# The eight constants of the 32nd-key pick move from the value products' PSUM bank to the score tile, and the pick moves one place forward

## The chip, the cores and the metric

The kernel runs on one core of one Trainium2 chip. Its engines are TensorE (PE in the profile; its weight loads are listed as PEld), VectorE (DVE), ScalarE (ACT), GpSimd (POOL) and SyncE (SP, which issues most DMAs). Each takes its own instructions in the order in which they were written and waits on semaphores for the others. The metric is the device time of one execution in microseconds (us), as the median over runs.

## The reference

Attention over 8 batches and 8 heads of 576 tokens with 64 dimensions, in which each query keeps its 32 best keys, and behind it a layer of 8 experts over the 4608 tokens:

```python
scores = scale * np.matmul(q, k.transpose(0, 1, 3, 2))
kth = np.partition(scores, -top_k, axis=-1)[..., -top_k:-top_k + 1]   # top_k = 32
scores = np.where(scores >= kth, scores, -1000000000.0)
attn = softmax(scores); attn_out = np.matmul(attn, v)
# then, for each token x: expert = argmax of cosine logits, gate = its softmax weight
out[mask] = gate_w[mask, None] * (np.maximum(x[mask] @ w1[e], 0.0) @ w2[e])
```

## The kernel before

The attention works in 32 units (a unit is one head of a pair of batches) of 9 tiles of 128 queries, 288 tiles in all, each against 576 keys. A loop (line 1026) writes out one iteration i for each tile, and every engine's order is that in which the loop writes. One tile passes through the engines over several iterations:

- `nat(i + 2)` (line 737): PE multiplies queries and keys of tile i+2 into the score tile `sc`, two PSUM banks of which columns 0 to 287 are written. There is one such tile. Right behind it `evac(i + 2)` (line 741) has ACT copy it to SBUF as `xs`.
- `groups(i)` and `chain(i - 1)` (lines 746, 754): DVE takes the eight largest of each of 8 groups of 72 scores (8 MAX8, line 750), and from these 64 the best 24 (lines 763 to 769, the last result is `z`).
- `sign1(i - 2)` (line 772): ACT compares all scores with the 24th value of the groups and counts, in `c1`, how many lie above it. `below(i - 2)` (line 779): POOL multiplies scores and signs into `y2`, where the values still to be searched are the largest.
- `select(i - 3)` (line 784), the pick: DVE takes the next eight from `y2` (line 789), and line 790 picks the one of them that is the 32nd key. To that end it compares `c1` with eight constants, `winp`, and adds up the products into `tall`.
- `sign2(i - 4)` (line 803): ACT compares the scores with the picked value; `offset(i - 5)` (line 813): DVE makes the mask `r` of it.
- `chunk` (line 823): for the unit before, PE computes the transposed scores of 128 keys in `pt` and adds the masks; ACT takes the exponential into `w` (line 859). `av` (line 862): PE multiplies one or two such `w` with the values, adding up in `po`, a PSUM bank of its own, in 6 of 9 iterations. `norm` (line 881): twice in 9 iterations ACT copies `po` to SBUF as `ob` (line 891).

Within iteration i ACT's order is: squares for the expert layer where there are any, `sign1`, `norm`'s copy, a copy of an expert block where there is one, `sign2`, `evac`, exponential. PE's is: `nat`, `chunk`, a small product for the expert logits in some, `av`, pieces of early expert blocks. DVE's is `offset`, then `groups` and `chain` taken in turn, the pick's two instructions set among them by the number `SEL`, as lines 1099 to 1107 say. A planner (SLOT and ROOM, lines 999 to 1013) hands PE, ACT and POOL additional pieces where it reckons them free; from about 390 us on it gives PE early expert blocks.

The eight constants are a DVE copy (line 612) from SBUF. Before, they lie in columns 400 to 407 of `po`, whose columns 0 to 364 hold the value products. The framework that sets the semaphores orders all accesses of a PSUM tile by different engines, of whatever columns, and reads among them.

After the last tile (at about 915 us) the experts' layer runs, 400 us of which the change touches no line.

Of the kernel before, what the change touches and what calls it, by code (L numbers as in the profile page):

```python
# [50 lines left out]
def attn_moe_kernel(ctx: ExitStack, tc: tile.TileContext, qk, vb, vt, emb, tau, w1, w2, out):  # L51
# [537 lines left out]
    with ExitStack() as sx:  # L589
# [14 lines left out]
        sc = ps_s.tile([P, 2, 512], F32, name="sc", tag="sc")  # L604
        po = ps_s.tile([P, 512], F32, name="po", tag="po")
# [2 lines left out]
                             start=(n == 0), stop=(n == WU - 1))  # L608
        pov = po[:, 0:5 * VW].rearrange("p (t e) -> p t e", t=5)

        winp = po[:, 400:408]
        nc.vector.tensor_copy(winp, win)

        NV = 2
# [382 lines left out]
            return out_  # L997

        SLOT = 2950
        SEL = 6  # L1000
        NOSC = (2, 3)
        SQN = 1
        SQX, SCX = 600, 0
# [22 lines left out]
        while i < ntile + 12 or sideq or later or bankq or early or squares or wq or mo["seg"] \  # L1026
# [73 lines left out]
            for n in range(8):  # L1100
                mix += ga[n:n + 1]
                mix += gb[n:n + 1]
                if n == SEL:
                    mix += gc[:1]
                if n == SEL + 1:
                    mix += gc[1:]
# [436 lines left out]
    with tc.If(fv > 0):  # L1543
        with ExitStack() as sx:
# [3 lines left out]
            with tc.For_i(0, NU, 1) as u:  # L1548
# [22 lines left out]
                for ti in range(9):  # L1571
                    sc = ps_1.tile([P, 2, 512], F32, name=f"gsc{ti}", tag="pt")
# [31 lines left out]
                    po = ps_1.tile([P, D], F32, name=f"gpo{ti}", tag="pa", bufs=1)  # L1604
# [86 lines left out]
```

## Time and profile before

| | us |
|---|---|
| median of 3 runs | 1333.33 (1330.56 to 1333.66) |
| profiled execution, device time | 1337.93 |
| its span, first to last instruction | 1336.1 |
| PE busy | 1266.3 (95%) |
| DVE busy | 1058.5 (79%) |
| ACT busy | 969.6 (73%) |
| POOL busy | 834.3 (62%) |

The shares are means over two different parts. Until about 915 us attention runs and DVE is busy nearly all the time; behind it DVE is mostly idle and PE carries the experts. A busy PE is a modelled figure, since matmuls overlap. The mean granted clock of TensorE was 0.982 of full speed.

### The profile page before, as it was taken

The numbers are of one execution on the slowest core, as the hardware profiler recorded it, in microseconds if no ns is written. First come the engines' busy times: TensorE is split into PE (matmuls) and PEld (weight loads), VectorE is DVE, ScalarE is ACT, GpSimd is POOL, SyncE is SP. The second block draws the span as 40 slices with busy tenths as digits, with TensorE's granted clock in tenths as the row PEclk, the third lists the DMA queues.
The fourth block names the chain that finished last, engine by engine and source line by source line (L and its number), as shares of the span: only waits on it lengthen the run. The fifth ranks groups of instructions, "written<-read, shape, count | busy, mean of one in ns | idle before, by whom it ended". The sixth has DMA issues, their size and how long they took to land. (4 is left out here: it accounts for less than half of the span.)

```text
span 1336.1 us, 40772 instructions
## 1 busy us (share of the span) xinstructions
PE 1266.3 (95%) x14044; PEld 1113.5 (83%) x14044; DVE 1058.5 (79%) x5829; ACT 969.6 (73%) x1890; POOL 834.3 (62%) x1343
## 2 busy tenths in 40 slices
PE   6999999999889999999999999998998999999997
PEld 4888888888788898988888898887797888888896
DVE  8999999999899999999999999998524234444240
ACT  5999999999889999988899998886414234433231
POOL 5678777889977778888878889955422211123011
PEclk7999999999999999999999999999998999999999
DMA  6477455564444665656666645624363344453211
GB/s 183 127 209 209 113 129 129 139 206 111 105 118 128 174 201 167 177 160 166 165 178 197 197 129 150 174 74 162 90 208 122 123 136 144 162 175 138 79 47 36
DMA packets 137107, 195.01 MB, mean 146 GB/s; under 512 B 63143, under 2 KB 63143, under 8 KB 136754
## 3 DMA queue, kind: packets, MB, share of 16 engines
q1 hardware_dynamic: 128562, 168.97, 44.7%
q0 software_dynamic: 8192, 22.07, 5.0%
q8 instruction: 132, 2.16, 0.7%
q14 instruction: 221, 1.81, 0.4%
HBM read 115.29 MB, written 20.87 MB: 102 GB/s over the span
## 5 line engine op out<-in xcount | busy, mean ns | idle before, releaser
L750 DVE MAX8 ca<-xs 128x8 f32<-128x72 f32 x2304 | 482.4, 220 | 1.4 <-ACT xs L743 1.2
L781 POOL TENSOR_TENSOR y<-xs,s 128x576 f32<-128x576 f32 x288 | 370.3, 1287 | 116.2 <-ACT s L775 55.0
L188 PE MATMUL sc<-st 128*128 128x288 f32 x1280 | 262.3, 332 | 32.0 <-ACT xs L743 28.4
L873 PE MATMUL po<-v,w 128*64 128x73 f32 (+1 forms) x5760 | 253.2, 231 | 4.5 <-DVE jk L790 1.8
L188 PEld LDWEIGHTS sc<-st 128*128 128x128 f32 x1280 | 186.3, 192 | 71.9 <-ACT xs L743 38.2
L873 PEld LDWEIGHTS po<-v,w 128*64 128x64 f32 (+1 forms) x5760 | 220.2, 136 | 25.3 <-ACT ob L891 2.8
L775 ACT ACTIVATE s<-xs,z 128x576 bf16<-128x576 f32 x288 | 224.3, 779 | 16.0 <-DVE z L769 9.2
L858 PE MATMUL pt<-st 128*128 128x288 f32 (+1 forms) x1280 | 224.3, 297 | 0.0
L789 DVE MAX8 z<-y 128x8 f32<-128x576 f32 x288 | 213.9, 743 | 0.3 <-POOL y L781 0.3
L810 ACT ACTIVATE s<-xs,tall 128x576 bf16<-128x576 f32 x236 | 183.4, 777 | 31.6 <-DVE jk L790 26.7
L859 ACT ACTIVATE w<-pt 128x576 f32<-128x576 f32 x288 | 189.4, 658 | 20.0 <-PE pt L858 17.0
L858 PEld LDWEIGHTS pt<-st 128*128 128x128 f32 (+1 forms) x1280 | 183.8, 184 | 1.1 <-ACT s L810 0.2
L743 ACT COPY xs<-sc 128x576 f32<-128x576 f32 x288 | 180.6, 627 | 4.6 <-PE sc L188 4.2
L858 PE MATMUL pt<-negi,r 128*128 128x128 bf16 (+4 forms) x1275 | 133.9, 209 | 5.2 <-DVE r L817 4.9
L413 POOL DMA_INDIRECT out_dram<-ys_w,wi x20 | 21.4, 1068 | 170.3 <-ACT ys_w L1262 62.0
L664 POOL TENSOR_TENSOR lo<-lo,hi 128x202 fp32r<-128x202 f32 x186 | 115.4, 621 | 15.5
L858 PEld LDWEIGHTS <-r 128*128 128x128 bf16 (+1 forms) x1920 | 103.6, 99 | 23.6 <-DVE r L817 6.6
L817 DVE TENSOR_SCALAR r<-s,top 128x576 bf16<-128x576 bf16 x236 | 119.9, 508 | 0.4 <-ACT s L810 0.4
L1243 PE MATMUL ph_w<-xTh,w 128*128 128x448 f32 (+3 forms) x384 | 99.0, 340 | 7.0 <-issue 7.0
L1258 PE MATMUL py_w<-w,hh 128*128 128x512 f32 x320 | 100.1, 394 | 0.8 <-ACT ys L1262 0.8
L1247 DVE SCALAR_TENSOR_TENSOR hl<-ph_w,hh 128x448 fp32r<-128x448 f32 (+3 forms) x48 | 25.9, 540 | 67.1 <-ACT hh L1246 66.8
L1243 PEld LDWEIGHTS ph_w<-xTh,w 128*128 128x128 f32 x384 | 70.6, 196 | 10.0 <-issue 8.2
(282 smaller groups left out, 2436.9 us busy)
## 6 DMA issues: line engine op xcount, KB each, us to landing
r<-in_w SPq DMA_DIRECT2D x128, 256.0 KB
fr<-in_w SPq DMA_DIRECT2D x28, 1024.0 KB
lo<-in_qk SPq DMA_DIRECT2D x62, 304.0 KB
st<-hi SPq DMA_DIRECT2D x124, 152.0 KB
st<-lo SPq DMA_DIRECT2D x124, 152.0 KB
v<-in_v SPq DMA_DIRECT2D x32, 288.0 KB
vt<-in_vt SPq DMA_DIRECT2D x32, 288.0 KB
st<-hi SPq DMA_DIRECT2D x62, 136.0 KB
```

The costliest lines, as they stand in the source:

```text
L188: nc.tensor.matmul(sc[:, hf, :SH], qs[:, cols(b)], kk[:, b * S + hf * SH:b * S + (hf + 1) * SH], start=(n == 0), stop=(n == len(terms) - 1))
L743: nc.scalar.copy(xs.rearrange("p (a b) -> p a b", a=2), sc[:, :, :SH])
L750: return [lambda gi=gi: nc.vector.max(out=ca[:, 8 * gi:8 * gi + 8], in_=xs[:, gi * GW:(gi + 1) * GW]) for gi in range(G)]
L775: nc.scalar.activation(s1, xss[i], AF.Sign, bias=zs[i][:, 15:16], scale=-SUCC, accum_out=c1)
L781: nc.gpsimd.tensor_tensor(y2, xss[i], s1s.pop(i), ALU.mult)
L789: lambda: nc.vector.max(out=z[:, 16:24], in_=y2),
L810: nc.scalar.activation(s2s[i], xss.pop(i).rearrange("p (a b) -> p a b", a=3), AF.Sign, bias=tall[:, i:i + 1], scale=-1.0)
L817: nc.vector.tensor_scalar(r, s2s.pop(i), BIG, tops[i // 9][:, i % 9, 0:1], op0=ALU.mult, op1=ALU.max)
L858: nc.tensor.matmul(o_, l_, r_, start=start, stop=stop)
L859: nc.scalar.activation(w.rearrange("p (a b) -> p a b", a=2), ps[:, :, :SH], AF.Exp, scale=0.125)
L873: nc.tensor.matmul(o, w[:, q:q + 64], vc, start=start and n < 2, stop=stop and n in (8, 7 - b))
L1243: nc.tensor.matmul(ph, w[:, c, f * P:(f + 1) * P], x[:, c, 0:n], start=(k == 0), stop=(k == len(terms) - 1))
```

## The change

The constants are copied into columns 400 to 407 of the second bank of the score tile `sc` (row length 512, of which the scores use 288), and line 790 reads them there. `SEL` falls from 6 to 5, so that both instructions of the pick stand one MAX8 earlier among DVE's. The whole diff:

```diff
@@ -608,7 +608,7 @@
         pov = po[:, 0:5 * VW].rearrange("p (t e) -> p t e", t=5)
 
-        winp = po[:, 400:408]
+        winp = sc[:, 1, 400:408]
         nc.vector.tensor_copy(winp, win)
@@ -997,7 +997,7 @@
         SLOT = 2950
-        SEL = 6
+        SEL = 5
         NOSC = (2, 3)
```

The order of DVE's instructions around the pick of tile 141 before (names end in the tile's number; `ca144` is the eight largest of the groups of tile 144, `z141` and `y2_141` belong to the pick, `r140` is a mask):

```order
L769 MAX z143_10206<-cb143_10205 128x8 [waits DVE_49]
L750 MAX ca144_10204<-xs144_10098 128x8 x2
L789 MAX z141_10081<-y2_141_10184 128x8 [waits Pool_49]
L750 MAX ca144_10204<-xs144_10098 128x8
L790 SCALAR_TENSOR_TENSOR jk141_10207,tall_167<-po_169,c1_141_10143,z141_10081 128x8 [waits DVE_49,PE_49]
L817 TENSOR_SCALAR r140_10275<-s2_140_10213,top15_9673 128x576 [waits Activation_49]
L750 MAX ca145_10270<-xs145_10151 128x8
```

The same place of DVE in the changed kernel:

```order
L769 MAX z143_10206<-cb143_10205 128x8 [waits DVE_49]
L750 MAX ca144_10204<-xs144_10098 128x8
L789 MAX z141_10081<-y2_141_10184 128x8 [waits Pool_49]
L750 MAX ca144_10204<-xs144_10098 128x8
L790 SCALAR_TENSOR_TENSOR jk141_10207,tall_167<-sc_168,c1_141_10143,z141_10081 128x8 [waits DVE_49,Activation_49]
L750 MAX ca144_10204<-xs144_10098 128x8
L817 TENSOR_SCALAR r140_10275<-s2_140_10213,top15_9673 128x576
```

One MAX8 has gone from ahead of the pick to behind it. The pick no longer waits for PE (the value products) but for ACT, and so late an instruction of ACT, the copy of the score tile in the same iteration, that the mask behind it needs no wait for ACT of its own.

PE's order where iteration 144 begins, before (`po` is written by the value products, `sc` by the scores, `pt15_0_0` by the transposed scores of unit 15):

```order
L873 MATMUL po_169<-v0_188,w14_1_1_10028 64x73 [waits DVE_49]
L873 MATMUL po_169<-v0_188,w14_1_1_10028 64x73 x8
L873 MATMUL po_169<-v0_188,w14_1_2_10100 64x73 [waits Activation_49]
L873 MATMUL po_169<-v0_188,w14_1_2_10100 64x73 x8
L188 MATMUL sc_168<-st16_9663 128x288 [waits Activation_49]
L188 MATMUL sc_168<-st16_9663 128x288 x3
L858 MATMUL pt15_0_0_10222<-st15_9051 128x288 [waits PE_49]
```

And in the changed kernel:

```order
L873 MATMUL po_169<-v0_188,w14_1_1_10028 64x73 x9
L873 MATMUL po_169<-v0_188,w14_1_2_10100 64x73 [waits Activation_49]
L873 MATMUL po_169<-v0_188,w14_1_2_10100 64x73 x8
L188 MATMUL sc_168<-st16_9663 128x288 [waits DVE_49]
L188 MATMUL sc_168<-st16_9663 128x288 x3
L858 MATMUL pt15_0_0_10222<-st15_9051 128x288 [waits PE_49]
```

No instruction moves on PE. The wait for DVE leaves the value products and stands at the scores, where it takes the place of the wait for ACT's copy of the tile before: the pick for which PE now waits is that of the iteration before, which itself waits for that copy. On ACT the order stays as well; `ob`, the copy of `po`, waits for PE instead of DVE, and `sign2` behind it takes over the wait for DVE.

## Rows read from the trace of the kernel before

**Rows 1.** Windows: length, then busy us of PE, PEld, DVE, ACT, POOL, granted clock.
```profile
100.00:420.00 320.00, 302.32 (x4579) 273.54 (x4579) 313.99 (x1973) 293.52 (x595) 267.14 (x459) 0.99 0.52 137
420.00:880.00 460.00, 454.61 (x5696) 393.78 (x5691) 456.81 (x2776) 417.94 (x824) 381.91 (x629) 1.00 0.62 171
```

**Rows 2.** Waits of DVE in 0 to 920 us: us in total, times, longest.
```profile
DVE jk L790 <- PE po L873: 4.4, 10, 1.0
...
DVE rd L897 <- POOL rd L895: 2.2, 1, 2.2
DVE jk L790 <- PE sc L188: 1.4, 3, 0.6
```

**Rows 3.** Waits of the whole span that the change touches on PE and ACT.
```profile
PEld sc L188 <- ACT xs L743: 38.2, 48, 2.3
...
ACT s L810 <- DVE jk L790: 26.7, 87, 1.1
...
ACT ob L891 <- DVE jk L790: 12.6, 34, 0.6
```

**Rows 4.** Timeline, five iterations of the scores' weight loads: start, us, instruction.
```profile
704.05 0.56 PEld L188 LDWEIGHTS sc<-st 128*128 128x128 f32 x4
707.01 0.56 PEld L188 LDWEIGHTS sc<-st 128*128 128x128 f32 x4
710.40 0.56 PEld L188 LDWEIGHTS sc<-st 128*128 128x128 f32 x4
713.61 0.56 PEld L188 LDWEIGHTS sc<-st 128*128 128x128 f32 x4
716.82 0.56 PEld L188 LDWEIGHTS sc<-st 128*128 128x128 f32 x4
```

**Rows 5.** Timeline of DVE: the pick of the same iterations, and a MAX8 before one.
```profile
704.63 0.21 DVE L790 SCALAR_TENSOR_TENSOR jk<-po,c,z 128x8 f32<-128x8 f32 x1
707.82 0.23 DVE L790 SCALAR_TENSOR_TENSOR jk<-po,c,z 128x8 f32<-128x8 f32 x1
710.97 0.23 DVE L790 SCALAR_TENSOR_TENSOR jk<-po,c,z 128x8 f32<-128x8 f32 x1
714.14 0.23 DVE L790 SCALAR_TENSOR_TENSOR jk<-po,c,z 128x8 f32<-128x8 f32 x1
717.10 0.22 DVE L750 MAX8 ca<-xs 128x8 f32<-128x72 f32 x1
717.23 0.21 DVE L790 SCALAR_TENSOR_TENSOR jk<-po,c,z 128x8 f32<-128x8 f32 x1
```

**Rows 6.** Timeline of ACT in the same stretch.
```profile
705.86 0.64 ACT L743 COPY xs<-sc 128x576 f32<-128x576 f32 x1
706.38 0.67 ACT L859 ACTIVATE w<-pt 128x576 f32<-128x576 f32 x1
706.92 0.65 ACT L327 ACTIVATE scra<-x 128x512 bf16<-128x512 f32 x1
...
707.54 0.79 ACT L775 ACTIVATE s<-xs,z 128x576 bf16<-128x576 f32 x1
...
708.30 0.78 ACT L810 ACTIVATE s<-xs,tall 128x576 bf16<-128x576 f32 x1
708.96 0.65 ACT L743 COPY xs<-sc 128x576 f32<-128x576 f32 x1
...
712.41 0.66 ACT L743 COPY xs<-sc 128x576 f32<-128x576 f32 x1
...
715.51 0.68 ACT L743 COPY xs<-sc 128x576 f32<-128x576 f32 x1
```

**Rows 7.** Timeline of PE: scores, end of the chunk, value products of one iteration.
```profile
716.85 0.77 PE L188 MATMUL sc<-st 128*128 128x288 f32 x4
...
718.24 0.19 PE L858 MATMUL pt<-negt,r 128*128 128x64 bf16 x1
...
718.37 1.48 PE L873 MATMUL po<-v,w 128*64 128x73 f32 x36
```

## The prediction

> **What bounds the kernel now.** I read the stretches first. Up to 920 us DVE sets the pace: in 100 to 420 us it is busy for 313.99 of 320 us, in 420 to 880 us for 456.81 of 460 [rows 1]. In the second stretch PE is as full, 454.61 us, so that two engines run there side by side without room; in the first PE has 17.7 us free. The list of DVE's waits then says what it still loses: four kinds of any size, of which the pick (line 790) waiting for PE makes 4.4 us in 10 waits and 1.4 us in 3 [rows 2]. The row that names the scores (sc) is the same wait, for the PE work in front of it, since the pick waits for value products alone. Last I set PE's, DVE's and ACT's timelines beside each other over five iterations at 704 to 718 us [rows 4 to 6]. Picks follow each other by 12.60 us in four iterations, 3.15 us each [rows 5]. What matters there is where an engine stands against the others: PE begins the scores of iteration i before DVE ends the pick of iteration i-1, by 0.79 us (704.05 against 704.84), 1.04, 0.80, 0.76 and 0.62, 0.80 in the mean [rows 4, 5].
>
> **The change part by part.** The sum is made against the profiled execution, 1337.93 us with a span of 1336.1; the median of the runs shown is 1333.33, so 4.6 us come off at the end.
>
> The copy of the constants at line 612 runs once and costs the same in either bank: nothing. Line 790 reads 8 columns of PSUM before and after: nothing on DVE. SEL moves one MAX8 behind the pick; MAX8 and pick start 0.13 us apart (717.10 and 717.23) [rows 5], the count is the same, and an independent MAX8 still stands between line 789 and line 790, so DVE's own time stays and the pick ends 0.13 us earlier against DVE's iteration.
>
> What goes: the pick's wait for the value products, 4.4 + 1.4 = 5.8 us [rows 2]. ACT's copy ob no longer waits for the pick, 12.6 us in 34 waits [rows 3]; that buys nothing by itself, because sign2 right behind it on ACT waits for the same pick, as it does 87 times now [rows 3], and ACT isn't the bound.
>
> What comes, first wait: the scores on PE wait for the pick of the iteration before. In each of the five iterations PE would have to start later, by 0.80 us in the mean, less the 0.13 by which the pick is earlier, some 0.7 us. Paid in each of 288 iterations that would be 200 us; that is the upper end and can't hold, because PE only comes to stand later beside DVE and then goes at DVE's pace. The lower end is nothing at all. The value is near the lower end: in the full stretch PE is never idle, so the largest of the gaps, 1.04 - 0.13 = 0.9 us, is paid once, and in the other iterations PE is then already later than the new wait wants. In the first stretch PE already stops at the same instruction for ACT's copy of the score tile (38.2 us in 48 waits over the span [rows 3]) and only stops for another reason. Queued behind the waiting scores are the chunk and the value products of the iteration, and for them ACT's exponential waits.
>
> What comes, second wait: the pick of iteration i waits for ACT's copy of the scores of the same iteration, which waits for PE. Today the copies end at 706.50, 709.61, 713.07 and 716.19, and the picks that will wait for them start at 707.82, 710.97, 714.14 and 717.23: 1.32, 1.36, 1.07 and 1.04 us in reserve, after SEL 0.13 less, so 0.91 at the least [rows 5, 6]. If PE starts 0.9 us later, the scores of 713.61 start at 714.5, end 0.8 us later [rows 7] at 715.3, and the copy that starts at 715.51 is not touched. The indirect way is longer. A chunk ends 1.6 us after the start of the scores (716.82 to 718.43 [rows 4, 7]); 0.9 us later, the chunk of 704.05 ends at about 706.6, and the exponential that starts at 706.38 is late by 0.2. From there ACT runs through without a gap to the next copy at 708.96, with an expert-layer square between (706.92) [rows 6], so the copy is late by 0.2 of 1.2 us. So in this stretch no pick stalls. But the reserve is spent by any iteration in which PE is late by another 0.5 to 1 us and ACT has a piece of 0.6 us more (line 327 of rows 6), and today's picks stall as well although they have a reserve. The bounds: nothing, and 145 iterations of the full stretch (460 / 3.15 makes 146) at the mean of today's stalls, 5.8 / 13 = 0.45 us, which is 65 us. I take one such stall for each unit of 9 iterations in the full stretch, the rate at which ACT's and PE's longest iterations of a unit can meet: 16 x 0.45 = 7.2 us. In the first stretch PE catches up in its free 17.7 us and I take none.
>
> The copy of ACT and the pick of DVE only read the score tile, and they wait for each other all the same; rows 3 show such a pair of reads today, ob and the pick in po, with 34 waits. The Trainium skill has this as a rule (PSUM — Partial Sum Buffer, section "PSUM bank collisions raise a hardware error"): engines are to be kept apart by bank and not by address, reads against reads included. The trace agrees, 12.6 us of ACT went into it. If columns alone decided, the constants at 400 and the scores up to 287 would not meet, no wait would come, and the sum would be the first rival's below.
>
> Sum: 1337.93 - 5.8 + 7.2 = 1339.3, and less 4.6 for the median: 1334.7 us. That is 0.1% over the time before. What is late next, once the pick waits for ACT, is ACT's way from the exponential to the score copy.
>
> **Rivals.** First: the new wait has reserve enough and only the old one goes. For it speak the five iterations above, in which no pick stalls, and that 1.04 us is more than the value products leave where two of them come together: they start at 718.37 and last 1.48 us [rows 7], which puts their end at 719.85 against the next pick at about 717.23 + 3.15 = 720.38, 0.5 us. Against it: PE's way to the reserve gets 0.9 us shorter, and PE in the full stretch has 5.4 us of 460 to make good lateness. It gives 1333.33 - 5.8 = 1327.5 us.
>
> Second, the other side: in the full stretch PE can't afford to be held. Mechanism: PE and DVE are both full there, and a wait for each other in each iteration, where today's wait stands in 6 of 9, takes away PE's freedom to start one iteration early and the next late. Place: the scores, line 188, from 420 us on. Price: the gaps between PE's start and the pick spread by 1.04 - 0.80 = 0.24 us from the largest to the mean; if PE is idle that long in each iteration and gets half of it back, 145 x 0.12 = 17 us are lost, less 5.8: 1333.33 + 11.6 = 1344.9 us. It decides from the point at which PE's idle time before the scores in 420 to 880 us exceeds the 5.4 us that PE has. For it speaks that PE has so little; against it that PE, once moved, has no reason to come early again.
>
> Third: the wait at the scores is worth more as an order than it costs. PE no longer runs ahead, and ACT's stops for the pick (26.7 us) [rows 3] turn into work; but DVE's busy time is the bound, and it has, beside the picks, only 2.2 us of waits for POOL in the attention loop [rows 2]. So this can't go below the first rival by more than about 2 us, 1325.
>
> **How the numbers follow.** The forecast gets 0.42, the first and third rival together 0.24, the second 0.34. Its 0.34 is high because I looked at five iterations of 288 and the price of a loop through three engines is seldom only the mean. About 0.3%, 4 us, is what a measurement of this kernel can tell from no change: 1329.3 to 1337.3. The first rival lies below, the second above, and the forecast's own range, 2 to 11 us for the new stalls, is 1330 to 1338. So faster 0.24, the same 0.42, slower 0.34. The range that holds the time 8 times in 10 goes from the first rival to a little above the second: 1327 to 1346.
>
> **What would show it right or wrong.** Right: in the profile after, DVE's waits at line 790 name ACT's copy (line 743) or PE in place of the value products, with 5 to 10 us in all; PE's scores start 0.05 to 0.5 us behind the pick in nearly all iterations of the full stretch; waits of the scores for ACT's copy are gone and waits for line 790 stand there, several tens of us in the first stretch; ob has no wait for DVE; DVE's busy time in 0 to 920 us is the same within 2 us. The first rival is right if line 790 waits for less than 2 us; the second if PE is idle before the scores by over 15 us between 420 and 880 us and picks there are more than 3.2 us apart. The forecast is wrong if DVE's own instructions take another time, if the picks stall by more than 12 us, or if the time moves behind 920 us, where the change touches nothing.

## The result, and the profile after

The changed kernel takes 1340.14 us (median of 9 runs, 1335.75 to 1342.86) against 1331.54 (9 runs, 1325.87 to 1333.66): a ratio of 1.0063, interval 1.0044 to 1.0082. It is slower by 8.6 us, more than the 0.3% that counts as no change. The prediction was 1334.7, in a range of 1327 to 1346.

Its profiled execution took 1342.58 us with a span of 1340.6, 4.5 us over that of before. The windows that answer to [rows 1]:

```profile
100.00:420.00 320.00, 298.69 (x4509) 268.56 (x4507) 310.62 (x1943) 286.00 (x589) 263.71 (x455) 0.99 0.53 139
420.00:880.00 460.00, 453.45 (x5674) 392.96 (x5670) 457.13 (x2769) 413.78 (x820) 384.22 (x635) 1.00 0.62 169
```

In the first stretch DVE, the pacing engine, gets 3.4 us less of work done in the same time, in the second it seems as full as before. The waits of DVE in 0 to 920 us (us in total, times, longest) answer to [rows 2]:

```profile
DVE jk L790 <- ACT xs L743: 9.5, 24, 0.7
```

and by stretch, the same list for 21 to 382 us and then for 382 to 930 us:

```profile
DVE jk L790 <- ACT xs L743: 8.1, 21, 0.6
```

```profile
DVE jk L790 <- ACT xs L743: 1.4, 3, 0.7
```

The pick's wait for the value products is gone; a wait for ACT's copy of the scores has come, nearly all of it ahead of 382 us. PE's and ACT's waits over the whole span answer to [rows 3]:

```profile
PEld sc L188 <- DVE jk L790: 58.6, 91, 2.8
...
PEld sc L188 <- ACT xs L743: 3.3, 4, 1.0
```

```profile
ACT w L859 <- PE pt L858: 44.3, 60, 2.4
...
ACT xs L743 <- PE sc L188: 33.1, 66, 1.3
...
ACT s L810 <- DVE jk L790: 1.5, 7, 0.3
```

PE now stops for the pick, and ACT, which used to stop for the pick, stops for PE: ACT's exponential (w) waited 17.0 us before and its copy of the scores (xs) 4.2.

To place the loss, I count by picks, not by the clock: the time from the first pick (tile 0) to those of tiles 20, 117 and 287, which holds the same work in each kernel. Tile 117 is where the light stretch ends (before 377.4 us, after 382.1).

| us | tiles 0 to 20 | 20 to 117 | 117 to 287 | behind the last pick |
|---|---|---|---|---|
| before | 59.8 | 295.7 | 536.9 | 421.8 |
| after | 61.7 | 299.1 | 539.6 | 418.9 |
| difference | +1.9 | +3.4 | +2.7 | -2.9 |

The picks take 8.1 us more, about the 8.6 of the medians. The last column holds only code that the change doesn't touch; over the profiles of the kernels below whose work there is whole it lies between 412.6 and 421.8 us, so the two spans alone, 4.5 us apart, hide half of the loss.

### The profile page after: what moved, and what is told of

It is laid out like the page before. It is cut to its first block, busy times and chain, and to the rows that moved or that the text cites. A ratio compares the mean times of both kernels' runs of the same rounds, so it can differ in the third digit from the quotient of the medians.

```text
span 1340.6 us, 40849 instructions
## 1 busy us (share of the span) xinstructions
PE 1266.1 (94%) x14044; PEld 1110.7 (83%) x14044; DVE 1061.7 (79%) x5829; ACT 962.3 (72%) x1890; POOL 834.4 (62%) x1343
## 5 line engine op out<-in xcount | busy, mean ns | idle before, releaser
L750 DVE MAX8 ca<-xs 128x8 f32<-128x72 f32 x2304 | 503.6, 221 | 0.6 <-ACT xs L743 0.6
L188 PE MATMUL sc<-st 128*128 128x288 f32 x1280 | 259.5, 329 | 43.5 <-DVE jk L790 36.5
L188 PEld LDWEIGHTS sc<-st 128*128 128x128 f32 x1280 | 185.2, 191 | 88.7 <-DVE jk L790 58.6
L743 ACT COPY xs<-sc 128x576 f32<-128x576 f32 x288 | 183.8, 639 | 37.7 <-PE sc L188 33.1
L817 DVE TENSOR_SCALAR r<-s,top 128x576 bf16<-128x576 bf16 x236 | 116.8, 495 | 0.6 <-ACT s L810 0.4
L546 DVE TENSOR_TENSOR w<-fr,w 128x512 fp32r<-128x512 f32 (+1 forms) x84 | 71.0, 865 | 7.7 <-ACT w L545 6.3
```

The source lines that it names most:

```text
L188: nc.tensor.matmul(sc[:, hf, :SH], qs[:, cols(b)], kk[:, b * S + hf * SH:b * S + (hf + 1) * SH], start=(n == 0), stop=(n == len(terms) - 1))
L743: nc.scalar.copy(xs.rearrange("p (a b) -> p a b", a=2), sc[:, :, :SH])
L750: return [lambda gi=gi: nc.vector.max(out=ca[:, 8 * gi:8 * gi + 8], in_=xs[:, gi * GW:(gi + 1) * GW]) for gi in range(G)]
L817: nc.vector.tensor_scalar(r, s2s.pop(i), BIG, tops[i // 9][:, i % 9, 0:1], op0=ALU.mult, op1=ALU.max)
```

## The experiments

The theory from the two profiles (the loop): the scores of iteration i wait for the pick of i-1, and that pick for the copy of the scores of i-1. Therefore PE can't run ahead of its heavy iterations, and where several follow each other, the pick stalls. Rivals: the place of the pick (SEL) costs the time; ACT's order is at fault; the value products' stretch (from tile 117 on) is where it is lost.

**The place alone, and the bank alone.** `e1_po_sel5` is the kernel before with the pick moved, `e2_sc_sel6` the kernel before with the constants moved:

```diff
-        SEL = 6
+        SEL = 5
```

> The second part of the change alone: the pick one place forward, the constants still in the value products' bank. Loop theory (the loss of 0.63% comes from the two new waits at the score tile): about the time before, ratio 0.998 to 1.002, the pick's waits name the value products (po) and stay at 4 to 8 us. Place theory (the loss comes from the earlier pick, which has 0.13 us less reserve and asks for POOL's y2 sooner): ratio 1.004 to 1.008, with DVE's waits at lines 789 and 790 above 9 us.

```diff
-        winp = po[:, 400:408]
+        winp = sc[:, 1, 400:408]
```

> The first part alone: constants in the score tile, the pick at its old place. Loop theory: slower than before, ratio 1.002 to 1.007; the pick's waits name ACT's copy of the scores (line 743); with 0.13 us more reserve, 24 waits of 9.5 us in all should shrink to 6 to 9 us, most of them before 420 us as in the changed kernel. Place theory: ratio 0.998 to 1.002, and those waits under 5 us.

Measured: 1331.64 against 1331.7 for the place, ratio 1.0003 (0.9989 to 1.0017); 1340.44 for the bank, 1.0067 (1.0044 to 1.009). The first list of DVE's waits is that of the place alone, the second that of the bank alone:

```profile
DVE jk L790 <- PE po L873: 5.3, 13, 0.9
```

```profile
DVE jk L790 <- ACT xs L743: 9.2, 23, 0.8
```

The bank costs all of it. The 0.13 us of reserve that the prediction took off for the place is worth nothing that can be seen: 9.2 us of stalls at the one place, 9.5 at the other. The expectation of the bank, 6 to 9 us, was just missed.

**No bank at all.** Line 790 reads the constants from SBUF, where `win` lies already, with SEL = 6 (`e3_sbuf_sel6`) and 5 (`e4_sbuf_sel5`):

```diff
-        winp = po[:, 400:408]
-        nc.vector.tensor_copy(winp, win)
+        winp = win
```

> The constants stay in SBUF and line 790 reads them there, so that the pick shares no PSUM bank with any engine; place as before. Loop theory: all waits of the pick for PE or for ACT's score copy go, 5 to 6 us, ratio 0.994 to 0.998 against before; the pick's own instruction stays at 0.22 us. Rival: reading three operands from SBUF makes line 790 dearer or the order of the engines without those waits is worse; ratio 1.000 to 1.006 and line 790 above 0.24 us, or new waits at line 789.

> Constants in SBUF and the pick one place forward. Loop theory: as the SBUF kernel with the pick at its old place, within 0.2% of it, since the place matters only through the waits at the bank. Place theory: 0.4 to 0.8% slower than that one.

Measured: 1339.38, 1.0061 (1.0042 to 1.0081), and 1336.35, 1.0027 (1.0012 to 1.0042). No pick waits for PE or ACT's copy, and both are slower than before, where I expected them faster. The reason stands in the row of the pick (line 789 there) of `e3_sbuf_sel6`: times, then ns least/median/longest.

```profile
L789 DVE SCALAR_TENSOR_TENSOR jk<-win,c,z x288: 198/213/1696, 21.6 to 920.5; 128x8 f32<-128x8 f32 x144
```

In the kernel before, line 790 takes 201/225/229 ns. With the constants in SBUF 73 of the 288 take over 0.3 us, 27.7 us more in all than at the median (68 and 24.8 us in `e4_sbuf_sel5`). The timeline of `e3_sbuf_sel6` (start, us, instruction) shows one:

```profile
309.40 0.63 POOL L663 TENSOR_TENSOR lo<-lo,hi 128x203 fp32r<-128x203 f32 x1
...
309.60 0.45 DVE L789 SCALAR_TENSOR_TENSOR jk<-win,c,z 128x8 f32<-128x8 f32 x1
```

The pick ends at 310.05, 0.02 us behind the end of POOL's instruction at 310.03. Of the 73 long ones 70 end within 0.05 us of the end of an instruction of POOL, 65 of these TENSOR_TENSOR; of the 215 others 39 do. The time by picks rose by 6.6 us (892.3 to 898.9). DVE was busy for 15.0 us more in it (882.2 to 897.2) and stood for 8.4 us less (10.2 to 1.7). So 12.7 of the 27.7 us came back in DVE's work: 152 picks have lost a separate wait instruction (53 have one in place of 205), which by an estimate from the spacings given below under line 790 is worth 0.07 to 0.10 us each, 11 to 15 us. These two runs took one wait away and put another in, and they leave the loop untested.

**ACT's order.** `e5_sc_copy_first` (the changed kernel) and `e6_po_copy_first` (the kernel before) put the scores and their copy ahead of `sign2` in the loop:

```diff
-            if ok(i - 4):
-                sign2(i - 4)
             if ok(i + 2):
                 nat(i + 2)
                 evac(i + 2)
+            if ok(i - 4):
+                sign2(i - 4)
```

> The changed kernel with ACT's order turned at one place: the copy of the new scores (line 743) stands ahead of sign2 instead of behind it. Loop theory (the lost time is a loop over two iterations: pick, scores, chunk, exponential, sign1, sign2, score copy, pick, that is longer than two short iterations of the first stretch): sign2's 0.7 us leaves the loop, so the pick's waits for line 743 fall from 9.5 us to under 3 us, and the last pick comes 4 to 8 us earlier than the 921.7 us of the changed kernel; ratio 0.999 to 1.004 against before. Rival (it is the wait on PE, scores behind the pick, which takes PE's time away whatever ACT does): waits before the scores stay and the last pick stays at 919 to 923 us, ratio 1.005 to 1.008.

> Control for the one before: the kernel before with the same turned order on ACT. Both theories: the pick does not wait for the copy there, so the order alone changes little; ratio 0.997 to 1.003, the pick's waits for the value products 4 to 8 us. If it gains as much as the changed kernel does from the same turn, the turn is good for another reason and says nothing on the loop.

Measured beside a before of 1334.91: `e5_sc_copy_first` 1345.8, 1.0081 (1.0064 to 1.0098); `e6_po_copy_first` 1331.64, 0.9971 (0.9956 to 0.9986), faster than either kernel. DVE's waits of `e5_sc_copy_first` in 0 to 930 us:

```profile
DVE jk L790 <- ACT xs L743: 8.2, 16, 1.6
DVE r L817 <- ACT s L810: 5.1, 18, 0.3
```

My number for `e5_sc_copy_first` failed: the last pick came at 929.1 us, later than in the changed kernel (921.7) and not earlier. Sorted by i mod 9, one kind of stall went all the same: in the changed kernel the picks between tiles 10 and 117 stall 5 times at i mod 9 = 5 (1.54 us) and 10 times at 7 (3.79 us); here those at 5 are gone, those at 7 stay (10 times, 4.49 us), and the mask (line 817), whose `sign2` now comes later, waits as well. So ACT's order is one of two ways to a stall, not the cause. In the kernel with the constants in `po` the same turn gains: PE runs further ahead (its scores begin in the mean 1.5 us ahead of the pick in the light stretch, 1.0 before), and the pick's waits for PE in 21 to 376 us shrink to one, of 0.2 us. By picks it gains 1.6 us of its 3.3; the rest lies behind the last pick, where the time varies anyway.

**Which stretch.** `e7_po_then_sc` reads the constants in `po` for tiles 0 to 116 and in `sc` from 117 on; `e8_sc_then_po` the other way round (SEL = 6 in both):

```diff
-        winp = po[:, 400:408]
-        nc.vector.tensor_copy(winp, win)
+        winp = po[:, 400:408], sc[:, 1, 400:408]
+        [nc.vector.tensor_copy(w_, win) for w_ in winp]
...
-                    jk, winp, c1, z[:, 16:24], op0=ALU.is_equal, op1=ALU.mult,
+                    jk, winp[i >= 9 * SHIFTED], c1, z[:, 16:24], op0=ALU.is_equal, op1=ALU.mult,
```

> Constants in both banks, the pick at its old place: for tiles 0 to 116 (short iterations, up to about 380 us) it reads the value products' bank, from tile 117 on the score tile. Loop theory: the first stretch goes as before (last pick of it at 377 to 379 us against 377.4 before and 382.1 changed), the second as in the changed kernel, where the pick's waits were 1.4 us against 3.1; ratio 0.996 to 1.001. Second rival of the prediction (the full stretch pays): ratio 1.004 to 1.008.

> The other way round: score tile for tiles 0 to 116, value products' bank from tile 117 on. Loop theory: all of the loss, pick 117 at 382 to 385 us as in the changed kernel, ratio 1.003 to 1.008, waits of the pick for line 743 of 7 us and more, all before 390 us. Second rival of the prediction: ratio 0.998 to 1.002.

Measured: 1335.78, 1.0006 (0.999 to 1.0022), and 1339.71, 1.0042 (1.0023 to 1.0061), with pick 117 at 378.7 and 383.9 us, both as the loop theory had it. The windows from pick 0 to 117 and from 117 to 287, columns as in [rows 1] (length, then busy us of PE, PEld and DVE), of the kernel before, the changed one, `e7_po_then_sc` and `e8_sc_then_po`:

```profile
21.93:377.38 355.45, 328.76 (x4953) 296.54 (x4954) 349.17 (x2199) 323.73 (x658) 289.39 (x491) 0.97 0.56 148
377.38:914.26 536.88, 527.66 (x6640) 457.26 (x6638) 533.00 (x3233) 486.19 (x951) 435.21 (x708) 1.00 0.58 160
```

```profile
21.26:382.08 360.82, 329.03 (x4904) 294.73 (x4904) 350.31 (x2199) 318.35 (x656) 289.43 (x491) 0.97 0.55 146
382.08:921.67 539.59, 530.84 (x6687) 459.55 (x6686) 535.28 (x3233) 483.89 (x954) 435.62 (x708) 1.00 0.58 160
```

```profile
22.32:378.68 356.36, 329.19 (x4936) 296.79 (x4936) 349.15 (x2199) 323.81 (x658) 290.02 (x491) 0.97 0.55 148
378.68:918.11 539.43, 529.45 (x6650) 458.02 (x6651) 535.46 (x3232) 482.56 (x951) 436.14 (x708) 1.00 0.58 160
```

```profile
21.64:383.88 362.24, 331.24 (x4941) 296.78 (x4942) 350.84 (x2199) 319.79 (x658) 289.32 (x491) 0.97 0.55 146
383.88:921.99 538.11, 529.10 (x6651) 458.68 (x6651) 533.50 (x3232) 485.61 (x951) 435.24 (x708) 1.00 0.58 160
```

Two things go with the constants' place. In the light stretch `sc` costs 6 to 7 us (362.24 against 356.36 and 355.45), mostly time in which DVE stands. And in either stretch DVE is busy longer with `sc` for the same instructions: 350.84 and 350.31 against 349.15 and 349.17, 535.46 and 535.28 against 533.50 and 533.00, that is 10 to 15 ns for each pick. Where this comes from stands below, under line 790.

**PE's burst.** In a unit of 9 iterations PE's heavy ones follow each other: i mod 9 = 4 has two chunks, 5 and 6 two sets of value products each (as have 3 and 8), 7 the scores of the next unit's first tile, 8 matmuls where others have 4. `e9_sc_less_burst` takes one set of value products out of this burst in the changed kernel, `e10_sc_less_free` one outside it; `e11_po_less_burst` and `e12_po_less_free` do the same to the kernel before.

```diff
-               6: [(1, 0, 1, 0), (1, 4, 0, 0)], 8: [(1, 1, 0, 0), (1, 2, 0, 0)], 0: [(1, 3, 0, 1)]}
+               6: [(1, 0, 1, 0)], 8: [(1, 1, 0, 0), (1, 2, 0, 0)], 0: [(1, 3, 0, 1)]}
```

```diff
-        AVS = {1: [(0, 0, 1, 0)], 3: [(0, 1, 0, 0), (0, 2, 0, 0)], 5: [(0, 3, 0, 0), (0, 4, 0, 1)],
+        AVS = {1: [(0, 0, 1, 0)], 3: [(0, 1, 0, 0)], 5: [(0, 3, 0, 0), (0, 4, 0, 1)],
```

> The changed kernel without one set of value products (the last 64 keys of the second batch, 0.7 us of PE), left out in the iterations i with i mod 9 = 6, which stand inside PE's run of heavy iterations (4 to 7: a double chunk, twice two sets of value products, the scores of a tile with twice as many matmuls). Read by the picks alone: from the first pick to that of tile 117 it took 360.8 us in the changed kernel, 355.5 before. Burst theory (a wait of the scores for the pick forbids PE to run ahead of its heavy iterations, and the pick at i mod 9 = 7 pays): the ten waits of 3.8 us at i mod 9 = 7 nearly vanish (under 1 us) and the stretch takes 356 to 358 us. Loop theory (ACT's sign2 in a loop of two iterations): waits at mod 5 (1.5 us) and mod 7 both stay, 359.5 us or more.

> The changed kernel with as much left out, but at i mod 9 = 3 (keys 256 to 383 of the first batch, 0.7 us of PE), ahead of the heavy iterations, where PE waits for the pick anyway. Burst theory: it helps little, since PE may not use the time: waits at mod 7 stay at 3 us or more, stretch 359 to 361 us. If PE's total work were what counts, it would gain as much as the one before.

> Control: the kernel before with the same left out at i mod 9 = 6. Both theories: PE can run ahead, so its waits fall a little; stretch 353 to 355.5 us. The difference between score tile and value products' bank, 5.3 us with all work, should be 1 to 3 us here by the burst theory, 4 to 6 by the loop theory.

> Control: the kernel before with the same left out at i mod 9 = 3. Here the time can be used in advance: stretch 353 to 355.5 us, so that the score tile costs 4 to 6 us against it by the burst theory, 1 to 3 if PE's total work were what counts.

Only the picks can be compared, since the left-out products change the experts' work behind them. Tiles 20 to 100, one profile each:

| us | in `sc` | in `po` | difference |
|---|---|---|---|
| whole | 243.9 | 239.8 | 4.1 |
| without one in the burst | 240.8 | 239.1 | 1.7 |
| without one outside it | 242.8 | 239.2 | 3.6 |

DVE's waits at line 790 between these picks, of the changed kernel, `e9_sc_less_burst` and `e10_sc_less_free`:

```profile
DVE jk L790 <- ACT xs L743: 5.9, 16, 0.6
```

```profile
DVE jk L790 <- ACT xs L743: 2.8, 8, 0.6
```

```profile
DVE jk L790 <- ACT xs L743: 4.0, 12, 0.6
```

From tile 10 to 117, without the product in the burst the ten stalls at i mod 9 = 7 are all gone and the five at 5 stay (1.57 us). Without one as long at i mod 9 = 3, nine of the ten stay (3.38 us), but four of the five at 5 go: these products stand right ahead of the double chunk. So it isn't PE's total work that decides but the work in a row just ahead of a stall.

The expectations named the whole way from tile 0 to 117. There the four kernels took 358.2, 362.7, 354.5 and 354.8 us; the first two are a little over what was expected (356 to 358, 359 to 361), the controls within it. So `sc` costs 3.7 us without the product in the burst and 7.9 without the other, against 5.4 whole, where the burst theory had 1 to 3 and 4 to 6: the order is as expected, the sizes are not. Part of the first excess lies in three stalls at tiles 4, 7 and 8, 2.4 us. The second kernel took 2.4 us more than the changed one between tiles 100 and 117: there PE had waited 2.2 us for a pick, the granted clock was 0.50 (1.2 of 2.4 GHz) from 353.4 to 358.2 us, the double chunk in it ended at 358.3, and the pick of tile 110 stood for 1.88 us.

## Why the prediction was right or wrong

**How a stall comes about.** The timeline of the changed kernel in the light stretch, one burst:

```profile
136.52 1.60 PE L873 MATMUL po<-v,w 128*64 128x73 f32 x36
...
137.10 0.23 DVE L790 SCALAR_TENSOR_TENSOR jk<-sc,c,z 128x8 f32<-128x8 f32 x1
...
138.05 0.80 PE L188 MATMUL sc<-st 128*128 128x288 f32 x4
...
139.71 1.64 PE L873 MATMUL po<-v,w 128*64 128x73 f32 x36
...
140.25 0.23 DVE L790 SCALAR_TENSOR_TENSOR jk<-sc,c,z 128x8 f32<-128x8 f32 x1
...
141.27 1.33 PE L188 MATMUL sc<-st 128*128 128x288 f32 x8
...
142.69 0.64 ACT L743 COPY xs<-sc 128x576 f32<-128x576 f32 x1 [0.81 <-PE sc L188]
...
143.36 0.23 DVE L790 SCALAR_TENSOR_TENSOR jk<-sc,c,z 128x8 f32<-128x8 f32 x1 [0.36 <-ACT xs L743]
```

The pick ends at 137.33 and at 140.48, but PE is still busy with two sets of value products and begins the scores 0.7 and 0.8 us later. The second time there are eight matmuls: the scores end at 142.60, the copy behind them at 143.33, and the pick has stood for 0.36 us. The same place before:

```profile
134.59 0.56 PEld L188 LDWEIGHTS sc<-st 128*128 128x128 f32 x4
...
135.06 0.23 DVE L790 SCALAR_TENSOR_TENSOR jk<-po,c,z 128x8 f32<-128x8 f32 x1
...
137.82 1.09 PEld L188 LDWEIGHTS sc<-st 128*128 128x128 f32 x8
...
138.23 0.23 DVE L790 SCALAR_TENSOR_TENSOR jk<-po,c,z 128x8 f32<-128x8 f32 x1
```

There PE came into the burst with a lead, and even at its end it begins 0.64 us before the pick ends (137.82 against 138.46). The new wait takes away the lead: between bursts PE has to stop for the pick. The other way to a stall (i mod 9 = 5) goes over ACT, again in the changed kernel:

```profile
105.64 0.69 PE L858 MATMUL pt<-st 128*128 128x288 f32 x4
...
106.54 0.71 PE L858 MATMUL pt<-st 128*64 128x288 f32 x4
...
107.79 0.65 ACT L859 ACTIVATE w<-pt 128x576 f32<-128x576 f32 x1 [1.26 <-PE pt L858]
...
108.34 0.77 ACT L775 ACTIVATE s<-xs,z 128x576 bf16<-128x576 f32 x1
...
109.10 0.77 ACT L810 ACTIVATE s<-xs,tall 128x576 bf16<-128x576 f32 x1
...
109.77 0.62 ACT L743 COPY xs<-sc 128x576 f32<-128x576 f32 x1
...
110.42 0.22 DVE L790 SCALAR_TENSOR_TENSOR jk<-sc,c,z 128x8 f32<-128x8 f32 x1 [0.24 <-ACT xs L743]
```

The double chunk, which PE begins late, ends at 107.8; from there exponential, sign1, sign2 and the copy follow without a gap, and the pick waits for the last. `e5_sc_copy_first` takes one link, sign2, out of this chain, and exactly these stalls go.

**Point by point.** The measured 1340.14 us lies within 1327 to 1346, but above the forecast's own 1330 to 1338 and among the slower times, which had a chance of 0.34. It is inside because the upper end was taken from the second rival, whose place was wrong: that is luck. The two waits were foreseen, and what they cost, and where, was not.

- The old wait goes (5.8 us): right, no pick waits for value products, and `ob` no longer waits for DVE. So are the waits that change hands: PE's 38.2 us for ACT's copy became 3.3, and 58.6 for line 790 stand there.
- The scores wait for the pick before, PE stands a little later and goes at DVE's pace in the full stretch: right. The scores' weight loads and the picks of the changed kernel answer to [rows 4, 5]:

```profile
709.39 0.23 DVE L790 SCALAR_TENSOR_TENSOR jk<-sc,c,z 128x8 f32<-128x8 f32 x1
...
709.79 1.08 PEld L188 LDWEIGHTS sc<-st 128*128 128x128 f32 x8
...
712.53 0.23 DVE L790 SCALAR_TENSOR_TENSOR jk<-sc,c,z 128x8 f32<-128x8 f32 x1
...
712.82 0.56 PEld L188 LDWEIGHTS sc<-st 128*128 128x128 f32 x4 [0.15 <-DVE jk L790]
...
715.74 0.23 DVE L790 SCALAR_TENSOR_TENSOR jk<-sc,c,z 128x8 f32<-128x8 f32 x1
...
716.02 0.56 PEld L188 LDWEIGHTS sc<-st 128*128 128x128 f32 x4 [0.33 <-DVE jk L790]
```

  PE stands 0.05 to 0.17 us behind the pick's end, 0.3 in the mean over the trace, and never ahead.
- New stalls, 16 times 0.45 us in the full stretch: wrong in place. Behind 382 us the picks wait for 1.4 us in 3 times; as the first rival had it, the reserve is enough there.
- "In the first stretch PE catches up in its free 17.7 us and I take none": this is the step that failed. The stalls are there, 8.1 us in 21 times, against 2.6 and 0.5 us of other waits of the pick in 21 to 378 us before. Free time that PE has as a sum is of no use to a burst if it can't be spent ahead of it, and the new wait forbids just that. DVE's iterations are also the shortest there: 295.7 us in 97 tiles before, 3.05 each, against 3.16 from tile 117 on, so that the same burst has less time.
- The second rival's mechanism, PE's freedom "to start one iteration early and the next late", is what happened, but not its place. In 420 to 880 us PE's weight loads, which run ahead, wait 15.8 us for the pick, just over the 15 that it named, but its matmuls only 5.3, and picks there follow each other by 3.17 us, not over 3.2. Its price, 11.6 us, was put together from the wrong stretch.
- "Line 790 reads 8 columns of PSUM before and after: nothing on DVE", "DVE's own time stays": wrong by 3.4 us, and so one of the prediction's own signs of being wrong came true. The lines of DVE up to the last pick, before and after (times, busy us, mean ns, idle before):

```profile
L790 DVE SCALAR_TENSOR_TENSOR jk<-po,c,z 128x8 f32<-128x8 f32 x288 | 63.7, 221 | 7.1 <-PE po L873 4.4 <-PE sc L188 1.4 <-ACT s L775 0.5
```

```profile
L790 DVE SCALAR_TENSOR_TENSOR jk<-sc,c,z 128x8 f32<-128x8 f32 x288 | 64.9, 225 | 10.1 <-ACT xs L743 9.5
```

  That is 4 ns in each pick, 1.2 us; from the first pick to the last DVE is busy for 3.4 us more (882.17 to 885.60), 12 ns in each of 288. It is not the bank but a wait that costs time without a stall. Ahead of a pick that waits for another engine the profile has a separate wait instruction, before in 205 picks, after in 283 (times, then ns least/median/longest):

```profile
L790 DVEq EVENT_SEMAPHORE  x205: 21/21/1079, 21.9 to 912.5; - x103
```

```profile
L790 DVEq EVENT_SEMAPHORE  x283: 21/21/21, 21.2 to 909.9; - x142
```

  In the kernel before, the 83 picks without it, nearly all at i mod 9 = 2, 4 and 7, where there are no value products, begin 134 ns behind the MAX8 ahead of them and take 209 ns, and the next instruction begins 135 ns behind them (medians). Of the 205 others 131 have 188, 226 and 151 ns, and the 74 that wait for three semaphores 216, 226 and 151. All of them read the same columns of `po`. In the changed kernel the 283 have 186, 225 and 151. The pick at 717.23 in [rows 5] is one without, 0.13 us behind its MAX8. That at 707.82 there is one with it, and so is that at 709.39 in the changed kernel, above; they stand 0.19 and 0.18 us behind these:

```profile
707.63 0.22 DVE L750 MAX8 ca<-xs 128x8 f32<-128x72 f32 x1
```

```profile
709.21 0.22 DVE L750 MAX8 ca<-xs 128x8 f32<-128x72 f32 x1
```

  So 78 picks became longer by 0.07 us and 74 shorter by 0.03: 5.5 - 2.2 = 3.3 us, against the 3.4 measured. The forecast's 0.13 us between MAX8 and pick was read from a pick without the wait.

The sum was 1.4 us over the time before, measured are 8.6. The picks' 8.1 us (892.33 to 900.41) divide by DVE's windows into 3.4 us of longer work, which the sum had at nothing, and 4.7 us in which DVE stands longer (10.2 to 14.8). Of these 3.0 stand ahead of line 790 (7.1 to 10.1 in the rows above), where the sum had 7.2 - 5.8 = 1.4, and 1.7 ahead of other lines. By stretches: 5.4 us up to tile 117, of which 1.1 are longer work; 2.7 behind it, of which 2.3 are. So only the time in which DVE stands is the loop's, and it is the larger part; the longer work is the price of the wait itself, which now comes in every iteration and not in about 7 of 10.

What stays open: whether the lower clock at the start has a part in the 1.9 us that the first 20 tiles lose (granted clock 0.84 there, 0.86 before; 1.8 us are stalls of the same kind), for which there is no run; and why the time behind the last pick varies by 9 us.

## What to carry to other kernels

A wait between two engines that are both in step costs little as long as neither needs its lead; so look for where the waiting engine has its heaviest iterations in a row, and whether it came into them ahead of the others. The free time of a stretch, as a sum, doesn't tell that: what does is the distance between two engines, iteration by iteration, ahead of the burst and at its end. A wait that never stalls isn't free either: here it made the pick and its neighbours 0.07 us longer on an engine that is full. Where a small constant lives in a bank of PSUM, it ties its reader to everyone who uses that bank; of the two banks tried here, the one that PE and ACT use in every iteration was the worse home for it.

## What the runs showed of the hardware

- A pick of 8 columns with all operands in SBUF took up to 1.70 us in place of 0.21, and nearly all the long ones end where an instruction of POOL ends; with one operand in PSUM none of 288 took over 0.23 us in the kernel before. The Trainium skill (SBUF — State Buffer, section "Who interferes with whom") has a rule for it: a DVE instruction with two inputs in SBUF and a GpSimd instruction that reads SBUF take the same read port, and the later one stands still until the other is done, while one with at most one SBUF input, outside the modes that use both ports, is not concerned. The traces agree on both sides: 73 of 288 held, for 27.7 us in all, in `e3_sbuf_sel6`, and none before. The constants' place in PSUM was thus worth more than the copy at line 612 shows.
- A separate wait instruction ahead of a DVE instruction cost time even where nothing stalled: in the kernel before, with the constants in one and the same place, the pick took 226 ns with it and 209 without, and began 188 ns behind the MAX8 ahead of it (216 with three semaphores) and not 134. The pick's mean of 225 ns in the score tile's bank against 221 in `po` is this and not the bank: with the wait it took 225 and 226 ns.
